# Outer-product recurrence and max-out layer on one core: another instruction order, two query steps in halves, one span turned by transfers

## The chip, the cores and the metric

The kernel runs on 1 core of one Trainium2 chip. The metric is the device time in microseconds (us) of one execution. The time of the kernel before is the median of three runs, 139.69 us (139.56 to 140.96).

## The reference

Two stages, one after the other. The first is a gated linear recurrence over 768 tokens for 4 batches, 8 heads and head size 48; the second is a max-out layer of 3072 tokens.

```python
f = 1.0 / (1.0 + np.exp(-f_logit))
for t in range(S):
    state = f[:, :, t, :, None] * state + np.einsum('bhd,bhe->bhde', k[:, :, t], v[:, :, t])
    y[:, :, t] = np.einsum('bhd,bhde->bhe', q[:, :, t], state)
x = y.transpose(0, 2, 1, 3).reshape(B * S, H * D)          # 3072 x 384
out = np.maximum(x @ w1, x @ w2) @ w_out                   # w1, w2 384 x 1024; w_out 1024 x 384
```

## The kernel before

The tokens are cut into 12 spans of 256 tokens: three windows of each of the four batches. Span s is window s // 4 of batch s % 4; a span is two chunks of 128 tokens, and each of the 128 partitions holds two neighbouring tokens ("parities"). Inputs of a span come as four loads of 384 KB (f, q, k, v) into 27 slots of SBUF. Spans 0 to 3 have no state at their start; later ones take the state of the span four before.

The max-out is rewritten: max(a, b) = b + relu(a - b). So the kernel forms wd = w1 - w2 once, and m2 = w2 @ w_out once; for each span it computes relu(x @ wd) @ w_out + x @ m2.

The whole program is one list of words, `ORDER`. A word is a step, its span or part, a letter for its engine where there is a choice (a ScalarE, v VectorE, p GpSimd, s SyncE) and after @ a PSUM bank or a slot. Each engine and each queue runs its own words strictly in the order in which they stand. Loads and stores all stand on SyncE's queue (SP). The words that matter here:

- Lf, Lk, Lq, Lv: the loads of a span. Wa0 to Wa3 (w1, 384 KB each), Wb0 to Wb2 (w2, 512 KB), Wo0 and Wo1 (w_out, 768 KB): the loads of the weights.
- E, F, G (ScalarE): gate, its logarithm, one factor. e: sum of a pair. C (TensorE): running sums. X and Z (ScalarE): the factors inv and dec. i, j: correction of the keys and the queries. K and Q: scaled keys (needs i and X) and queries (needs j and Z). V: values as bf16.
- t and u (TensorE): 16 transposes each, of the keys and of the queries; U: their copy out of PSUM (tile trs). A: scores of a half of the heads; m (VectorE): the masked scores. S and y: the outputs from the state and from within the span; z: a short read that keeps order. D, n, N: the state's update.
- Y: the outputs as bf16. For spans 6 to 10 (`TURNED`) Y goes to the tile xr, which has one buffer, and M turns it with a DMA transpose into xT. d: a quarter of x @ wd, 6 matmuls; r: relu; o: half of the output tokens, 11 matmuls over the rows of m2 and w_out; b: its copy out of PSUM; O: the store.
- wc, wt, wx: w2 as bf16, transposed, copied out. ws: a quarter of wd (needs a Wa and all three Wb). wo: a quarter of w_out as bf16. wm, wn: m2 and its copy. g: a memset of a state buffer.

Some rows of the profile have the line of a helper: L114 is the copy used by U, V, Y, b, wc, wx, wo and wn. Others: L247 step_i, L251 step_j, L258 step_K, L261 step_Q, L275 the transposes, L292 step_A, L299 step_m, L314 and L323 S and y, L387 step_D, L404 and L409 n and N, L427 step_M, L436 step_d, L461 step_o, L503 wm, L511 ws.

Of the kernel before, what the change touches and what calls it, by code (L numbers as in the profile page):

```python
# [12 lines left out]
BF16 = mybir.dt.bfloat16  # L13
# [7 lines left out]
Lf0s@16 g0v Lf1s@17 Lq0s@18 Lk0s@19 Lk1s@20 Lv0s@21 Lq1s@22 Wa2s E0 Wb1s F0 Lv1s@23 E1 e0v C0@0 F1  # L21
Wb2s j0v Z0 e1v X0 Q0v G0 C1@1 Wb0s i0v X1 u0@2 G1 g2v K0v Lf2s@24 i1p t0@2 U0.0v@2 U0.1a@3 Wa0s V0v
Z1 K1v D0@2 A0.1@0 Wa3s j1v A0.0@4 Q1v Wa1s m0.1v@0 u1@6 t1@6 Wo0s n0.0v U1.0a@6 U1.1a@7 Wo1s V1v
n0.1v D1@0 m0.0v@4 S0.0@2 A1.0@6 Lk2s@25 wc2a z0v@2 m1.0v@6 A1.1@4 S0.1 y0 Lq2s@26 wc0a ws2p n1.0v
n1.1v m1.1v@4 S1.0@6 Y0.0a@2 wt2@0 Lf3s@16 E2 g5p z1v@6 N1.1v S1.1 y1 N0.1p Lv2s@17 g3p ws0v wt0@1
Y1.1a@7 wx2a@0 Y0.1v@3 wc1p Lq3s@18 Y1.0v@6 d0.2@2 F2 g1p ws3v d0.0@4 Lk3s@19 wx0a@1 wt1@0 g4v e2v
d0.3@3 ws1v C2@1 r0.1a@2 d1.2@6 Lf4s@21 wo0v wx1v@0 wo1p d0.1@5 G2 d1.3@7 r0.0v@4 d1.0@2 Lv3s@20
wo2p wo3a d1.1@3 r1.1v@6 Z2 wm0@0 X2 g6v Lk4s@22 r1.0a@2 i2v wm1@1 K2v Lf5s@23 j2v wm2@2 Q2v Lq4s@24
E3 wn1v@1 t2@4 u2@4 F3 U2.0v@4 Lf6s@12 V2p wn2a@2 wn0v@0 o0.1@1 U2.1v@5 e3p A2.1@2 Lq5s@13 b0.1.0a@1
D2@4 A2.0@6 G3 n2.0v C3@0 j3v o1.1@1 Z3 n2.1v Lk5s@0 i3v X3 Q3v o1.0@0 m2.1v@2 E4 K3p F4 m2.0v@6  # L30
# [12 lines left out]
A7.0@0 b4.0.0v@2 A7.1@4 D7@6 N5.1p m7.0v@0 o5.0@3 Lq11s@19 K8p Lk11s@20 n7.0v O3.2s m7.1v@4 C9@2
N7.0p b5.0.0a@3 t8@0 Z9 u8@0 N6.1v S7.0@4 V8v X9 o5.1@3 U8.2v@0 V9a F11 n7.1v i9v D8@2 b5.1.0a@3
A8.1@0 z7v@4 N7.1p A8.0@6 n8.0v E10 m8.1v@0 d6.2@2 K9p d6.3@3 m8.0v@6 d6.0@0 r6.1a@2 N8.0p d6.1@1
Q9v S8.0@2 r6.0a@0 S7.1 y7 z8v@2 j11v t9@6 u9@6 e11v Y7.2a@4 S8.1 y8 U9.2v@6 C11@0 G11 M7s o6.1@1
F10 i11p Z11 Lk10s@23 X11 Q11p o6.0@4 Y8.2a@2 e10p A9.0@6 b6.0.0a@4 D9@0 M8s A9.1@2 K11p n9.0v
d7.1@5 m9.1v@2 C10@0 O5.2s d7.0@4 Z10 m9.0v@6 Lq10s@22 b6.1.0a@1 d7.3@3 Lv11s@12 G10 d7.2@2 O4.2s
r7.0a@4 N9.0v i10p Lv10s@24 d8.3@7 O6.2s X10 d8.1@5 r7.1a@2 K10v d8.2@6 d8.0@4 r8.1a@6 o7.1@1
r8.0a@4 j10v Q10p S9.0@2 t11@4 t10@6 z9v@2 u11@4 S9.1 y9 U11.0v@4 u10@6 U11.1v@5 o7.0@0 U10.2a@6  # L50
V11v V10v b7.1.0v@1 o8.1@4 Y9.2a@2 b7.0.0a@0 M9s D10@1 b8.1.0a@4 D11@0 O7.2s A11.0@2 A10.0@6 n11.0v
A11.1@4 m10.0v@6 o8.0@0 m11.1v@4 d9.0@6 N11.0v n10.0v d9.1@7 m11.0v@2 N10.0p d9.3@5 r9.0a@6 d9.2@4
b8.0.0v@0 O8.2s S10.0@0 r9.1a@4 S11.0@2 z10v@0 A10.1@6 z11v@2 S11.1 y11 m10.1v@6 S10.1 y10 Y11.0a@2
Y11.1a@3 o9.0@4 Y10.2a@0 M10s d11.2@5 b9.0.0v@4 d11.1@0 d11.3@1 o9.1@4 d10.1@3 b9.1.0v@4 r11.4a@5
# [6 lines left out]
M2_LAST = (0,)  # L61
TURNED = (6, 7, 8, 9, 10)


@with_exitstack
def kernel(
# [21 lines left out]
    DP = 64  # L88
# [174 lines left out]

    def step_V(s, e):
        copy(e, pad("vb", s)[:, :, :, 0:D], by_parity(loaded[s]["v"]))


    def transposes(s, x, b):
        src = pad("kpqp"[2 * x:2 * x + 2], s)
        for j in range(NP):  # L270
            for par in range(2):
                for h in range(2):
                    rows = slice(h * HC, (h + 1) * HC)
                    ps = banks16[:, b + h, :].rearrange("p (x j a t) -> p x j a t", x=2, j=NP, a=2)
                    nc.tensor.transpose(out=ps[:, x, j, par, :],  # L275
                                        in_=src[rows, par, 2 * j:2 * j + 2, :].rearrange("p r e -> p (r e)"),
                                        identity=ident[rows, rows])

    def step_U(s, part, e, b):
        t = tr[s] = buf("trs", s, 3, [C, 2, 2, NP, 2, HC], BF16)  # L280
        hs = slice(0, 2) if part == 2 else slice(part, part + 1)
        copy(e, t[:, hs].rearrange("p h x j a t -> p h (x j a t)"), banks16[:, b:b + hs.stop - hs.start, :])

    def step_A(s, jj, b):
        t = tr[s]
        for j in range(2 * jj, 2 * jj + 2):
            for par in range(2):
                for h in range(2):
                    for r in range(2):
                        rows = slice(r * DP, r * DP + D)  # L290
                        ps = banks[:, b + r, :].rearrange("p (j a t) -> p j a t", j=2, a=2)
                        nc.tensor.matmul(out=ps[h * HC:(h + 1) * HC, j % 2, par, :],  # L292
                                         lhsT=t[rows, h, 0, j, par, :],
                                         rhs=t[rows, h, 1, j].rearrange("p a t -> p (a t)"),
                                         start=True, stop=True, skip_group_check=True)
# [31 lines left out]
    def step_S(s, part, b):  # L327
        t = tr[s]
        if s in TURNED:
            ys[s] = b if part == 0 else ys[s]  # L330
            for j in range(NP):
                for r in range(2):
                    h = r if part else 1 - r
                    if has_state(s, h):
                        rows = slice(r * DP, r * DP + D)
                        add_turned(s, h, 2 * j + r, t[rows, h, 1, j].rearrange("p a t -> p (a t)"),
                                   heads_of(state_before(s, h))[rows, j, :], False)
            return
# [129 lines left out]
    def step_O(g, part):  # L468
# [3 lines left out]
        if g in TURNED:  # L472
            dst = out[row:row + W, :].rearrange("(h t a) m -> a t h m", h=2, a=2)
            for a in range(2):
                nc.sync.dma_start(out=dst[a], in_=obs[g][a * HC:(a + 1) * HC])
            return
        if g == n_s - 1 and part > 0:
            cols = slice((part - 1) * HD // 2, part * HD // 2)
            nc.sync.dma_start(out=dst[:, 1, cols], in_=obs[g][:, 1, cols])
            return  # L480
        pars = slice(0, 2) if part == 2 else slice(part, part + 1)
        nc.sync.dma_start(out=dst[:, pars, :], in_=obs[g][:, pars, :])
# [26 lines left out]
    def subtract(part, e):  # L509
# [15 lines left out]
        "t": lambda s, e, b: transposes(s, 0, b), "u": lambda s, e, b: transposes(s, 1, b),  # L525
        "U": lambda s, i, e, b: step_U(s, i, e, b),
# [3 lines left out]
        "Y": lambda s, i, e, b: step_Y(s, i, e, b), "g": lambda i, e, b: step_g(i, e), "M": lambda s, e, b: step_M(s, e),  # L530
        "D": lambda s, e, b: step_D(s, b),
# [3 lines left out]
        "O": lambda s, i, e, b: step_O(s, i),  # L535
# [4 lines left out]
    }  # L540
    for word in ORDER.split():
# [32 lines left out]
```

## Time and profile before

| | |
|---|---|
| median of three runs | 139.69 us |
| the profiled execution's own time | 141.23 us |
| its span | 139.5 us |
| TensorE busy | 119.1 us (85%) |
| VectorE busy | 101.7 us (73%) |
| ScalarE busy | 79.0 us (57%) |
| GpSimd busy | 45.3 us (32%) |
| read from HBM, written | 23.59 MB, 4.72 MB |
| granted TensorE clock | 1.0 throughout |

The span runs from the first to the last record of the profile; the execution's own time has 1.7 us more around it, and the profiled execution is 1.5 us above the median of the runs without a profile. TensorE's busy share counts overlapping matmuls as one stretch.

### The profile page before, as it was taken

The page shows a single profiled execution, that of the slowest core. Times are in us where ns is not written, and L with a number is a line of the kernel's source. Part 1 is how long each engine was busy: PE and PEld are TensorE (multiplying, and loading weights), DVE is VectorE, ACT ScalarE, POOL GpSimd, SP SyncE. Part 2 cuts the span into 40 slices and gives each one's busy share as a digit, 9 for nine tenths or more (in the row PEclk, how much of TensorE's full clock was granted, in tenths as well). Part 3 has the DMA queues.
Part 4 walks back from the last instruction along what each step waited for, and adds up shares of the span by engine and source line. Part 5 has one row for each costly group of instructions (what it writes and reads, how often), then busy time and mean ns, then how long its engine had stood idle before and what let it go on. Part 6 is the DMA issues. An engine that isn't in the chain of part 4 may idle for free. (4 is left out here: it accounts for less than half of the span.)

```text
span 139.5 us, 5551 instructions
## 1 busy us (share of the span) xinstructions
PE 119.1 (85%) x2455; PEld 89.5 (64%) x2455; DVE 101.7 (73%) x173; ACT 79.0 (57%) x120; POOL 45.3 (32%) x52
## 2 busy tenths in 40 slices
PE   0045489599999999999999699989999999999991
PEld 0024377586567687677787566776877668778671
DVE  5687798999889999989974989982642768312630
ACT  3784349665592996973983355693675814504301
POOL 5003007640538224482073096719635001000000
PEclk9999999999999999999999999999999999999999
DMA  4999999999999989999999999909899461422124
GB/s 109 271 261 296 348 332 349 369 267 251 269 265 257 271 222 273 239 248 250 247 297 222 224 274 163 288 30 96 121 260 313 130 140 34 118 56 61 57 62 164
DMA packets 59768, 29.65 MB, mean 213 GB/s; under 512 B 54368, under 2 KB 58592, under 8 KB 59744
## 3 DMA queue, kind: packets, MB, share of 16 engines
q1 hardware_dynamic: 59744, 29.30, 87.5%
q8 instruction: 19, 0.31, 1.0%
q14 instruction: 5, 0.04, 0.1%
HBM read 23.59 MB, written 4.72 MB: 203 GB/s over the span
## 5 line engine op out<-in xcount | busy, mean ns | idle before, releaser
L436 PE MATMUL banks<-xT,wd 128*128 128x256 bf16 x288 | 34.7, 273 | 2.3 <-DVE xT L114 2.0
L461 PE MATMUL banks<-wo,gT 128*128 128x384 bf16 (+1 forms) x200 | 35.3, 320 | 0.0
L436 PEld LDWEIGHTS <-wd 128*128 128x128 bf16 x288 | 27.2, 98 | 6.9 <-issue 2.3
L445 ACT ACTIVATE gT<-banks 128x1024 bf16<-128x1024 f32 (+1 forms) x20 | 19.5, 982 | 20.2 <-PE banks L436 15.7
L299 DVE TENSOR_TENSOR at_m<-banks,mask 128x1024 bf16<-128x1024 f32 x24 | 28.8, 1218 | 0.8 <-PE banks L292 0.5
L461 PEld LDWEIGHTS <-gT 128*128 128x128 bf16 x200 | 19.2, 98 | 11.8
L247 POOL TENSOR_TENSOR slots<-slots,one 128x384 f32<-128x384 f32 x8 | 8.5, 1058 | 28.1 <-DMA slots<-in_k_dram 18.3
L461 PE MATMUL banks<-m,xT 128*128 128x384 bf16 (+1 forms) x75 | 15.9, 320 | 0.0
L114 ACT COPY ob<-banks 128x384 f32<-128x384 f32 (+1 forms) x16 | 7.4, 460 | 11.9 <-PE banks L461 11.9
L114 DVE COPY trs<-banks 128x2048 bf16<-128x2048 bf16 (+1 forms) x12 | 11.9, 997 | 2.4 <-PE banks L275 2.3
L213 ACT ACTIVATE gate<-slots 128x768 f32<-128x768 f32 x12 | 10.1, 841 | 5.0 <-DMA slots<-in_f_logit_dram 5.0
L114 DVE COPY ob<-banks 128x384 f32<-128x384 f32 x9 | 5.0, 555 | 8.9 <-PE banks L461 8.9
L228 PE MATMUL banks<-e,u_inc 128*128 128x384 bf16 x12 | 4.2, 354 | 8.0 <-DVE e L224 8.0
L258 POOL TENSOR_TENSOR kp<-slots,inv 128x768 bf16<-128x768 f32 x5 | 9.6, 1913 | 3.0 <-DVE slots L247 2.9
L404 DVE TENSOR_TENSOR tmp_s<-banks,state 128x192 f32<-128x192 f32 x16 | 5.6, 352 | 6.7 <-ACT ob L114 3.9
L217 ACT ACTIVATE ell<-gate 128x768 f32<-128x768 f32 x12 | 10.1, 845 | 0.2
L292 PE MATMUL banks<-trs 48*64 48x128 bf16 x384 | 10.1, 234 | 0.0
L261 POOL TENSOR_TENSOR qp<-slots,dec 128x768 bf16<-128x768 f32 x4 | 7.3, 1817 | 8.3 <-PE banks L314 4.9
L251 DVE SCALAR_TENSOR_TENSOR slots<-gate,slots 128x384 f32<-128x384 f32 x12 | 6.6, 552 | 3.9 <-DMA slots<-in_q_dram 3.9
L114 ACT COPY trs<-banks 128x1024 bf16<-128x1024 bf16 (+1 forms) x4 | 4.8, 1227 | 7.0 <-PE banks L275 7.0
L292 PEld LDWEIGHTS <-trs 48*64 48x64 bf16 x384 | 7.5, 115 | 1.6 <-issue 1.1
L461 PEld LDWEIGHTS <-xT 128*128 128x128 bf16 x75 | 6.5, 97 | 3.2
(73 smaller groups left out, 186.3 us busy)
## 6 DMA issues: line engine op xcount, KB each, us to landing
slots<-in_f_logit_dram SPq DMA_DIRECT2D x12, 384.0 KB, 6.4
slots<-in_q_dram SPq DMA_DIRECT2D x12, 384.0 KB, 6.2
slots<-in_k_dram SPq DMA_DIRECT2D x12, 384.0 KB, 6.1
slots<-in_v_dram SPq DMA_DIRECT2D x12, 384.0 KB, 5.8
out_dram<-ob SPq DMA_DIRECT2D x6, 384.0 KB, 3.9
out_dram<-ob SPq DMA_DIRECT2D x11, 192.0 KB, 3.4
slots<-in_moe_w_dram SPq DMA_DIRECT2D x4, 384.0 KB, 8.7
slots<-in_moe_w_dram SPq DMA_DIRECT2D x3, 512.0 KB, 8.8
```

Source lines behind the costliest of these rows:

```text
L114: (nc.scalar.copy if e == "a" else engines[e].tensor_copy)(out, in_)
L213: nc.scalar.activation(flat(gate[s]), flat(loaded[s]["f"]), AF.Exp, bias=0.0, scale=-1.0)
L217: nc.scalar.activation(flat(ell[s]), flat(gate[s]), AF.Ln, bias=1.0, scale=1.0)
L247: engines[e].tensor_mul(even, even, one[s])
L251: engines[e].scalar_tensor_tensor(out=even, in0=gate[s][:, :, 1, :], scalar=1.0, in1=even, op0=ALU.add, op1=ALU.mult)
L258: engines[e].tensor_mul(pad("kp", s)[:, :, :, 0:D], by_parity(loaded[s]["k"]), both(inv[s]))
L261: engines[e].tensor_mul(pad("qp", s)[:, :, :, 0:D], by_parity(loaded[s]["q"]), both(dec[s][:, 0:HD].rearrange("p (h d) -> p h d", h=H)))
L292: nc.tensor.matmul(out=ps[h * HC:(h + 1) * HC, j % 2, par, :], lhsT=t[rows, h, 0, j, par, :], rhs=t[rows, h, 1, j].rearrange("p a t -> p ( ...
L299: nc.vector.tensor_mul(at[s][:, jj].rearrange("p r j a t -> p (r j) (a t)"), banks[:, b:b + 2, :].rearrange("p r (j x) -> p (r j) x", j=2) ...
L436: nc.tensor.matmul(out=ps[:, f], lhsT=wd[:, kt, ff * C:(ff + 1) * C], rhs=xT[g][:, kt], start=(kt == 0), stop=(kt == KT - 1))
L445: nc.scalar.activation(dst, src, AF.Relu)
L461: nc.tensor.matmul(out=ps, lhsT=lhs, rhs=rhs, start=(i == 0), stop=(i == len(terms) - 1))
```

## The change

`ORDER` is written anew, and some words are new.

- Spans 0 and 1: step Q on all eight heads becomes two steps q of four heads each (q0.0, q0.1, q1.0, q1.1), the transposes u become uq (8 each), and the copy U has the parts 3 (all keys), 4 and 5 (the queries of half the heads).
- Span 11: t11, u11 and both U11 are gone. Mk11 and Mq11 turn its scaled keys and queries with a DMA transpose each (128 x 1024, bf16) from SP's queue straight into trs; `key_t` and `query_t` hand the turned pieces to A and S.
- A step on GpSimd of the kinds in `SHARED` waits for the last such step of VectorE that stands ahead of it in the list.
- The stores O7, O8, O9 and the last piece of O11 are issued by ScalarE.
- Everything has a new place, and many steps another engine. Word for word, GpSimd loses four e, three i, two K, three Q and three V, and takes one K, two Q, two V, one q, five N (against three), a ws, and more g.

```diff
+SHARED = ("e", "i", "j", "K", "Q", "q", "V", "N", "ws", "wc", "wo")
 TURNED = (6, 7, 8, 9, 10)
+BY_DMA = (11,)
...
+    def step_q(s, jj, e):
+        hs = slice(4 * jj, 4 * jj + 4)
+        sums = dec[s][:, 0:HD].rearrange("p (h d) -> p h d", h=H)[:, hs]
+        engines[e].tensor_mul(pad("qp", s)[:, :, hs, 0:D], by_parity(loaded[s]["q"])[:, :, hs],
+                              sums.unsqueeze(1).to_broadcast([C, 2, 4, D]))
...
+        if part > 2:
+            x, js = (0, slice(0, NP)) if part == 3 else (1, slice(2 * part - 8, 2 * part - 6))
+            src = banks16[:, b:b + 2, :].rearrange("p h (x j y) -> p h x j y", x=2, j=NP)
+            copy(e, t[:, :, x, js].rearrange("p h j a t -> p h (j a t)"),
+                 src[:, :, x, js].rearrange("p h j y -> p h (j y)"))
+            return
...
+    def step_turn(s, x, e):
+        t = tr[s] = buf("trs", s, 3, [C, 2, 2, NP, 2, HC], BF16)
+        src = pad("kpqp"[2 * x:2 * x + 2], s).rearrange("p two h e -> p (two h e)")
+        engines[e].dma_start(out=whole(t)[:, x], in_=src, transpose=True)
...
+    def key_t(s, rows, h, j, par):
+        if s in BY_DMA:
+            return whole(tr[s])[rows, 0, NP * par + j, h * HC:(h + 1) * HC]
+        return tr[s][rows, h, 0, j, par, :]
...
-                nc.sync.dma_start(out=dst[a], in_=obs[g][a * HC:(a + 1) * HC])
+                engines[e].dma_start(out=dst[a], in_=obs[g][a * HC:(a + 1) * HC])
...
+        if key in SHARED and e in ("v", "p"):
+            ins = nc.cur_bb.bb.instructions[-1]
+            if e == "v":
+                ahead = ins.name
+            elif ahead:
+                tc.add_manual_dep(ins, ahead, mybir.DependencyInfo(mybir.DependencyClass.Sync,
+                                                                   mybir.DependencyReason.DATA),
+                                  reason="as listed")
```

The parts of the two lists that the prediction speaks of, taken apart by engine:

```
SP before:  f0 f1 q0 k0 k1 v0 q1 Wa2 Wb1 v1 Wb2 Wb0 f2 Wa0 Wa3 Wa1 Wo0 Wo1 k2 q2 f3 v2 ...
SP after:   f0 f1 k0 Wb2 q0 q1 v0 f2 Wb0 Wb1 k1 Wa1 Wa0 v1 Wa3 Wa2 Wo1 f3 Wo0 q2 k2 v2 ...
            ... M6 v10 k11 v11 v9 M7 q10 M8 Mq11 O4 Mk11 O6 M9 O5 M10 O10 O11.0 O11.1
PE before:  C0 C1 u0 t0 D0 A0 A0 u1 t1 D1 S0.0 A1 A1 S0.1 y0 S1.0 wt2 S1.1 y1 wt0 d0.2 d0.0
            wt1 d0.3 C2 d1.2 d0.1 d1.3 d1.0 d1.1 wm0 wm1 wm2 t2 u2 ...
PE after:   C0 t0 wt2 C1 uq0.0 uq0.1 A0 A0 uq1.1 uq1.0 D0 S0.0 S0.1 y0 wt0 t1 wt1 C2 A1.1 d0.0
            d0.1 A1.0 D1 d0.3 S1.0 S1.1 y1 d0.2 d1.3 d1.1 d1.2 d1.0 C3 wm2 wm1 wm0 u2 t2 ...
            ... y7 S8.1 y8 o6.0 C10 o6.1 C11 d7 D9 A9 A9 o7.0 d8 S9.0 u10 t10 S9.1 y9 o7.1
            A10.1 D11 A11.1 A10.0 D10 o8.0 d9 ...
DVE after:  ... m0.1 q1.1 m0.0 n0.0 z0 n0.1 K1 U1.4 ws1 e2 ws0 Y0.0 wx1 m1.1 m1.0 n1.0 n1.1 z1
            wo2 Y1.0 e3 wo0 r0.1 j2 Q2 i2 K2 U2.1 ...
ACT after:  ... U0.5 U0.4 Z1 X1 E2 U1.5 F2 Y0.1 wc1 U1.3 wx0 r0.0 Z2 G2 X2 Y1.1 E3 F3 wo1 ...
            ... X10 Z10 Y8 Z11 b6.1 X11 r7.1 ...
POOL after: g5 g2 g0 q1.0 g6 g4 wc0 i1 N0.1 V1 ws3 ws2 wo3 Q3 ... i11 K11 Q10 N9.0 N11.0
```

More of the change, by code (lines that the diff above doesn't have):

```diff
@@ L26 @@
[L26 to L30, printed above, removed]
@@ L43 @@
[L43 to L48, printed above, removed]
@@ L49 @@
[L49 to L54, printed above, removed]
@@ new lines @@
+i11p S7.1 y7 S8.1 y8 U9.2a@6 N7.1v e10v o6.0@4 Y7.2v@2 e11v M7s i10v C10@5 o6.1@2 V10v X10 Lq10s@24
+j11v Z10 K10v C11@3 b6.0.0v@4 V9v Y8.2a@0 d7.3@7 d7.2@6 Z11 M8s b6.1.0a@2 Q11v d7.0@0 X11 r7.1a@6
+d7.1@1 K11p Mq11s D9@2 r7.0a@0 A9.1@4 A9.0@6 o7.0@3 O4.2s j10v Mk11s m9.1v@4 Q10p d8.3@1 O6.2s
+m9.0v@6 d8.2@0 d8.0@4 n9.0v r8.1a@0 N9.0p d8.1@5 S9.0@0 r8.0a@4 u10@6 t10@6 z9v@0 V11v S9.1 y9
+U10.2a@6 o7.1@2 Y9.2v@0 M9s b7.0.0a@3 A10.1@0 b7.1.0v@2 D11@3 A11.1@4 O5.2s A10.0@6 n11.0v O7.2a
+D10@2 m10.1v@0 N11.0p o8.0@3 m11.1v@4 d9.2@0 n10.0v m10.0v@6 d9.1@5 d9.3@1 d9.0@4 r9.1v@0 o8.1@2
@@ L466, in step_b, with step_O @@
         copy(e, obs[g][:, par, cols], banks[:, b, cols])
-    def step_O(g, part):
+    def step_O(g, part, e):
         w, b = divmod(g, B)
@@ L525 @@
         "t": lambda s, e, b: transposes(s, 0, b), "u": lambda s, e, b: transposes(s, 1, b),
+        "uq": lambda s, i, e, b: transposes(s, 1, b, range(2 * i, 2 * i + 2)),
+        "q": lambda s, i, e, b: step_q(s, i, e),
         "U": lambda s, i, e, b: step_U(s, i, e, b),
@@ L540 @@
     }
+    ahead = None
     for word in ORDER.split():
```

94 lines of the change are left out of this document (59 added, 35 removed).

## The prediction

> **What bounds the kernel now.** I read the page first, then the busy time of four stretches of the span, then the timeline of the first 37 us.
>
> ```profile
> span 139.5 us, 5551 instructions
> PE 119.1 (85%) x2455; PEld 89.5 (64%) x2455; DVE 101.7 (73%) x173; ACT 79.0 (57%) x120; POOL 45.3 (32%) x52
> ```
>
> ```profile
> 0.00:27.00 27.00, 12.12 (x349) 10.47 (x350) 21.61 (x51) 16.23 (x22) 7.77 (x18) 1.00 1.07 289
> 27.00:36.50 9.50, 9.50 (x109) 7.16 (x108) 9.08 (x15) 5.78 (x9) 2.12 (x3) 1.00 1.08 271
> 36.50:136.60 100.10, 97.47 (x2000) 71.85 (x1998) 70.98 (x109) 56.64 (x90) 35.36 (x32) 1.00 0.83 189
> 136.60:139.50 2.90, 0.00 (x0) 0.00 (x0) 0.00 (x0) 0.31 (x1) 0.00 (x0) 1.00 0.36 129
> ```
>
> The columns are stretch, length, then busy time of PE, PEld, DVE, ACT, POOL, the granted clock, the DMA share and GB/s. TensorE is idle for 14.9 of the first 27 us, then works without a gap until 36.5 and loses only 2.6 us in the 100 us after that. The last 2.9 us are one copy and the last store. In the first 27 us the transfers are never idle (share 1.07). So the time is: when TensorE gets going, plus its own work, plus small gaps, plus the tail. An edit counts if it lets TensorE do more before about 30 us, takes work off TensorE later, or opens or closes gaps. TensorE enters its unbroken stretch so:
>
> ```profile
> 25.83 1.47 PE L436 MATMUL banks<-xT,wd 128*128 128x256 bf16 x12 [1.64 <-DVE xT L114]
> ...
> 28.51 3.43 PE L436 MATMUL banks<-xT,wd 128*128 128x256 bf16 x30
> 31.78 4.06 PE L503 MATMUL banks<-wo,slots 128*128 128x384 bf16 x24
> ```
>
> The thirty matmuls at 28.51 are d1.2, d0.1, d1.3, d1.0 and d1.1, 0.114 us each; the last row is the product m2. If d0.1 (0.69 us) had been done ahead, as in the new order, span 1's d steps would have begun at 29.2. That is the mark which the new order has to meet.
>
> **The start, step by step.** When loads land is read from the steps that waited for them:
>
> ```profile
> 7.46 0.56 DVE L251 SCALAR_TENSOR_TENSOR slots<-gate,slots 128x384 f32<-128x384 f32 x1 [0.70 <-DMA slots<-in_q_dram]
> 10.60 1.15 POOL L247 TENSOR_TENSOR slots<-slots,one 128x384 f32<-128x384 f32 x1 [8.06 <-DMA slots<-in_k_dram]
> 21.48 1.04 ACT L114 CAST slots<-slots 128x1024 bf16<-128x1024 f32 x1 [0.28 <-DMA slots<-in_moe_w_dram]
> 24.18 1.03 DVE L511 TENSOR_TENSOR wd<-slots 128x768 bf16<-128x768 f32 x1 [0.47 <-DMA slots<-in_moe_w_dram]
> 28.39 0.84 POOL L114 CAST wo<-slots 128x768 bf16<-128x768 f32 x1 [1.84 <-DMA slots<-in_moe_w_out_dram]
> 30.49 0.83 ACT L114 CAST wo<-slots 128x768 bf16<-128x768 f32 x1 [0.61 <-DMA slots<-in_moe_w_out_dram]
> ```
>
> From q0 (7.46) to k1 (10.60) two loads of 384 KB landed, 1.57 us each; from Wo0 (28.39) to Wo1 (30.49) one of 768 KB, 2.1 us. The new order keeps the volume and changes who comes first. k1 was fifth and lands eleventh: through k1 the queue now holds what the old one held through Wb0 (21.48), with f2 in place of v1 and without Wa2, so it lands one load earlier, about 20.2. By adding single loads from the start it would be 19.2. Wo0 now lands last, after f3: one load after 30.49, about 32.0.
>
> What follows k1 is a chain on three engines: i1 on GpSimd (1.15, in the row of 10.60), K1 on VectorE, then VectorE's words in their order. GpSimd has wc0 ahead of i1, and that waits for Wb0, so i1 ends no earlier than about 20.9; with k1 at 20.2 it is 21.4. I take K1's start at 21.2. VectorE's durations:
>
> ```profile
> L258 DVE TENSOR_TENSOR kp<-slots,inv 128x768 bf16<-128x768 f32 x7 | 6.6, 945 | 1.1 <-POOL slots L247 1.0
> L224 DVE TENSOR_TENSOR e<-ell 128x384 bf16<-128x384 f32 x6 | 3.2, 541 | 0.8 <-ACT ell L217 0.8
> L114 DVE COPY slots<-banks 128x1024 bf16<-128x1024 bf16 x1 | 0.7, 678 | 0.0
> L299 DVE TENSOR_TENSOR at_m<-banks,mask 128x1024 bf16<-128x1024 f32 x24 | 28.8, 1218 | 0.8 <-PE banks L292 0.5
> L404 DVE TENSOR_TENSOR tmp_s<-banks,state 128x192 f32<-128x192 f32 x16 | 5.6, 352 | 6.7 <-ACT ob L114 3.9
> L114 DVE CAST wo<-slots 128x768 bf16<-128x768 f32 x1 | 1.2, 1175 | 0.0
> L114 DVE CAST m<-banks 128x384 bf16<-128x384 f32 x2 | 1.1, 550 | 0.0
> ```
>
> ```profile
> 41.31 2.35 DVE L299 TENSOR_TENSOR at_m<-banks,mask 128x1024 bf16<-128x1024 f32 x2
> ```
>
> K1 0.95; U1.4, half of a copy of 1024, 0.4 (between 0.34 and 0.68 by the copy row); ws1 and ws0 1.03 each; e2 0.54; Y0.0 0.55 (the copy of 384 values from PSUM); wx1 0.68; m1.1 and m1.0 1.22 each; n1.0 and n1.1 0.35 each; wo2 1.18; Y1.0 0.55: together 10.1. Two m back to back take 2.35 and not 2.44, so each step but the last saves 0.09, about 1.1 over thirteen. Y1.0 ends at 21.2 + 9.0 = 30.2, and d1 starts there against the mark of 29.2: **1.0 us lost**. With K1 at 20.9 it is 0.7; if a weight load holds up ws1 or ws0 it is 2. Nothing else TensorE has in its order covers it: d0.0, d0.1, A1, D1, y1 and d0.2 are done by then, and m2 stands behind d1.
>
> The halved queries do work: the first half of span 0 is turned before the second is scaled, so span 0's outputs come earlier. But d0 stands on TensorE behind t1 and A1.1, which hang on k1, so that lead goes into waiting, and I cost it at nothing; at best it makes up the 1.0.
>
> d1 is done at 30.2 + 24 x 0.114 = 32.9, and C3 stands between it and m2 (moved from behind m2, so not added). wo0 needs Wo0 at 32.0 plus its cast of 1.18: 33.2. So m2 starts with no or little wait, 0.1; if f3 costs more than one load, a wait of up to 1 us.
>
> **Later parts.** Taking t11 and u11 off TensorE is read from the chain that ended last, and so is the price of a DMA transpose:
>
> ```profile
> 93.56 3.95 DMA xT<-xr
> ...
> 98.43 3.77 DMA xT<-xr
> ...
> 102.25 2.79 PE banks L436 x24
> 105.04 1.79 PE banks L461 x11
> ...
> 107.03 0.70 PE banks L275 x48
> ```
>
> Forty-eight transposes took 0.70, so thirty-two give back **0.5 us**. The U11 copies leave VectorE, which is not the bound there. Against it stand two more transfers on SP, 1024 columns where M7 and M8 had 768, so by 4/3 of 3.8 about 5 us from issue to landing. They must land before A11.1. Counted from M7's landing: TensorE has d7 and d8 (2.8 each), o7.0 and o7.1 (1.8 each) and about 2.6 us of D9, A9, S9, u10, t10, y9, A10.1 and D11 ahead of A11.1, 11.8 us. Mk11 waits for Y8, Z11, b6.1 and X11 on ScalarE, then K11 on GpSimd:
>
> ```profile
> L114 ACT CAST xr<-banks 128x768 bf16<-128x768 f32 x4 | 3.2, 803 | 2.1 <-DMA xT<-xr 2.1
> L243 ACT ACTIVATE dec<-banks 128x392 f32<-128x392 f32 x12 | 5.9, 494 | 2.5 <-PE banks L231 2.5
> L258 POOL TENSOR_TENSOR kp<-slots,inv 128x768 bf16<-128x768 f32 x5 | 9.6, 1913 | 3.0 <-DVE slots L247 2.9
> ```
>
> 0.8 + 3 x 0.5 + 1.9 = 4.2, and 5 to land: 9.2, with 2.6 to spare. I cost the transfers at nothing; SP carries M8, Mq11 and O4 ahead of Mk11, and that is the slow rival. d7 itself waits for M7: o6.0 and o6.1 (3.6) with S8, y8 and two C, about 5, stand against Y7 (0.95, as K of the same size) and 3.9 of transfer; I add 0.3, between 0 and 1.
>
> **The waits of GpSimd** have a reason in the trace:
>
> ```profile
> 51.46 1.03 POOL L247 TENSOR_TENSOR slots<-slots,one 128x384 f32<-128x384 f32 x1 [4.18 <-DMA slots<-in_k_dram]
> 51.54 1.16 DVE L409 TENSOR_TENSOR state<-tmp_s,dec 128x192 bf16<-128x192 f32 x1
> ```
>
> ```profile
> L409 DVE TENSOR_TENSOR state<-tmp_s,dec 128x192 bf16<-128x192 f32 x9 | 5.1, 568 | 0.0
> ```
>
> That N, a small product, took 1.16 us and ended just after GpSimd's step; undisturbed it is near the 0.35 of n. Over nine N that is 2.0 us of VectorE. The Trainium skill (GPSIMD Engine Reference, section Key points) says that GpSimd shares its SBUF interfaces with VectorE and contends with VectorE instructions that have two SBUF inputs; this row agrees. By it alone the waits would give VectorE up to those 2.0 us. Since TensorE is busy 97.5 of 100.1 us beside it, I take none of it, and bound the gain by the 2.6 us of gaps, the loss by as much again: a GpSimd step now queued behind a late VectorE step delays its followers (K after i, then t).
>
> The stores moved to ScalarE: it was busy 57%, and the last store still begins after the last copy. I cost them at nothing. The Trainium skill (Trainium Kernel Development and Optimization, section Key Constraints) has it that issuing from several engines only saves the sequencer's issue time; no run here shows that yet.
>
> **The sum** against the profiled span: 139.5 + 1.0 + 0.1 - 0.5 + 0.3 = 140.4. The profiled execution's own time is 141.23, 1.5 above the median of the runs without a profile; I put the difference, +0.9, on the median 139.69: **140.6 us**.
>
> **The rivals.**
> - *Faster, 137.4.* The d1 mark is met (k1 earlier, or wc0 quicker: the 1.0 and 0.1 are gone), the transposes give 0.5, and the 2.0 us of contention on VectorE closes most of the 2.6 us of gaps, 1.8. 139.69 - 2.3 = 137.4. For it: VectorE is busy 9.1 of 9.5 us where TensorE starts. Against: in the 100 us after, only 71 of 100.
> - *Slower, 142.7, span 11's transfers.* If a transpose holds SP's transfers for its whole time to landing, M8 lands 4.7 after M7, Mq11 9.7, O4 10.9, Mk11 16, and A11.1, with o8 and d9 behind it in TensorE's order, waits 4.2 us. Half of that, for transfers that overlap in part, gives 140.6 + 2.1 = 142.7. It decides from the point where Mk11 lands later than 11.8 us after M7.
> - *No change, 139.7.* The waits bind nowhere since GpSimd is behind anyway, the new order only trades gaps, and start and transposes cancel.
>
> **How the numbers follow.** Forecast 0.43 (own range 139.5 to 142.0), faster 0.22, span 11 late 0.20, no change 0.15. A measurement of this kernel tells about 1% from no change: below 138.3 and above 141.1. Faster: 0.20 of the second, 0.02 each of forecast and no change, 0.24. Slower: all of span 11 late, 0.14 of the forecast (its upper part, a weight load that holds up ws), 0.02 of no change, 0.36. The rest, 0.40, is within 1%. The range reaches to the faster case and past the slow one, 137.4 to 143.5.
>
> **What would show it.** Right: d1 and m2 start 1 us later than now, GpSimd's step_i at about 20 us waits for k1's load, no gap ahead of A11.1, TensorE's gaps after 37 us again near 2.6 us. Wrong: d1 at 29 or earlier; VectorE's state products at 0.35 us and gaps well under 2 us; or a gap of over 1 us that ends with trs from a DMA.

## The result and the profile after

The changed kernel is a little slower: 141.90 us median of 15 runs (140.66 to 143.25) against 140.52 us (139.11 to 141.96, 15 runs) of the kernel before on the same chip. The ratio is **1.0107 [1.0078, 1.0136]**. The forecast was 140.6 us, a loss of 0.9 us on the 139.69 us it started from; the ratio makes it 1.5. The ratios here and below leave out executions that are more than 1.5% above the fastest of the same kernel.

The page of the kernel after, its span and engines, and the busy time of the four stretches that were shown of before (same columns):

```profile
span 139.4 us, 5485 instructions
PE 119.8 (86%) x2423; PEld 89.0 (64%) x2423; DVE 100.8 (72%) x174; ACT 85.3 (61%) x126; POOL 36.5 (26%) x47
```

```profile
0.00:27.00 27.00, 13.23 (x303) 10.56 (x304) 20.91 (x51) 14.41 (x22) 10.30 (x23) 1.00 1.06 286
27.00:36.50 9.50, 8.37 (x116) 6.16 (x116) 6.05 (x12) 6.35 (x12) 2.32 (x2) 1.00 1.11 277
36.50:136.60 100.10, 98.21 (x2006) 72.30 (x2004) 73.79 (x113) 64.54 (x95) 23.93 (x23) 1.00 0.84 195
136.60:139.50 2.90, 0.00 (x0) 0.00 (x0) 0.00 (x0) 0.03 (x1) 0.00 (x0) 0.99 0.29 100
```

The first thing to see is that the spans hide the loss: 139.4 after, 139.5 before. The profile of before that the prediction was built on came from an execution 1.5 us above its median, with gaps at 78 and 93 us of 0.71 and 0.52 that a second profile of the same kernel does not have. That second one has a span of 137.9, a second one of after again 139.4, and their difference, 1.5, is near that of the medians, 1.4. So before and after are compared from here on by the second profiles, *before again* and *after again*.

The loss lies ahead of 36.5 us: by 27.0 TensorE has passed 303 matmuls instead of 349, and in the second stretch, where it had 9.50 us of work in 9.50, it now has 8.37. The timeline of TensorE in *before again*, where it enters the product m2 and where it ends:

```profile
28.26 3.44 PE L436 MATMUL banks<-xT,wd 128*128 128x256 bf16 x30
31.53 4.06 PE L503 MATMUL banks<-wo,slots 128*128 128x384 bf16 x24
...
134.17 0.82 PE L461 MATMUL banks<-wo,gT 128*128 128x192 bf16 x8
```

The same in *after again*:

```profile
30.07 0.52 PE L344 MATMUL banks<-at_m,vb 64*64 64x128 bf16 x18 [0.73 <-issue]
34.14 4.06 PE L541 MATMUL banks<-wo,slots 128*128 128x384 bf16 x24
...
135.44 0.82 PE L499 MATMUL banks<-wo,gT 128*128 128x192 bf16 x8
```

m2 starts at 34.14 instead of 31.53, **2.6 us later**; 0.3 of that is C3, which now stands ahead of it. From m2 to the end of the last matmul it is 102.1 us instead of 103.5 (135.44 + 0.82 - 34.14 against 134.17 + 0.82 - 31.53), so **1.3 come back**. The tail is 3.1 instead of 2.9. The sum is 2.6 - 1.3 + 0.2 = 1.5.

The first row of after again is what no part of the prediction had: in the middle of y1, between two matmuls of the same step, TensorE stood for 0.73 us, and the profile names no releaser ("issue"). The experiments ask where the 2.6 us come from, whether the waits of GpSimd and span 11's transfers cost or give anything, and what that stop is.

### The profile page after: what moved, and what is told of

It is laid out like the page before. It is cut to its first block, busy times and chain, and to the rows that moved or that the text cites. A ratio compares the mean times of both kernels' runs of the same rounds, so it can differ in the third digit from the quotient of the medians.

```text
span 139.4 us, 5485 instructions
## 1 busy us (share of the span) xinstructions
PE 119.8 (86%) x2423; PEld 89.0 (64%) x2423; DVE 100.8 (72%) x174; ACT 85.3 (61%) x126; POOL 36.5 (26%) x47
## 4 chain that ended last, share of the span: by engine, by line
PE 72%; DVE 9%; DMA 6%; ACT 6%; issue 3%; POOL 1%; DVEq 0%; POOLq 0%
PE banks L499 25%; PE banks L474 23%; PE banks L344 6%; PE banks L283 4%; PE banks L323 4%; DMA xT<-xr 3%; PE banks L352 3%; DMA slots<-in_f_logit_dram 3%; PE banks L425 2%; PE banks L541 2%; DVE trs L116 2%; PE banks L529 1%; DVE kp L260 1%; POOL qp L263 1%; ACT ell L219 1%
## 5 line engine op out<-in xcount | busy, mean ns | idle before, releaser
L499 PEld LDWEIGHTS <-gT 128*128 128x128 bf16 x200 | 19.2, 98 | 11.8
L116 ACT COPY trs<-banks 128x2048 bf16<-128x2048 bf16 (+2 forms) x10 | 13.0, 1314 | 5.8 <-PE banks L283 5.8
L485 DVE TENSOR_SCALAR gT<-banks 128x1024 bf16<-128x1024 f32 x5 | 6.1, 1219 | 6.1 <-PE banks L474 6.0
L263 POOL TENSOR_TENSOR qp<-slots,dec 128x768 bf16<-128x768 f32 x3 | 5.4, 1816 | 17.6 <-DVE slots L253 12.5
L116 DVE COPY ob<-banks 128x384 f32<-128x384 f32 (+1 forms) x10 | 5.3, 534 | 6.1 <-PE banks L499 6.1
L260 POOL TENSOR_TENSOR kp<-slots,inv 128x768 bf16<-128x768 f32 x4 | 7.3, 1815 | 9.5 <-DVE qp L263 7.0
L260 DVE TENSOR_TENSOR kp<-slots,inv 128x768 bf16<-128x768 f32 x8 | 7.9, 991 | 1.0 <-POOL slots L249 0.4
L344 PE MATMUL banks<-at_m,vb 64*64 64x128 bf16 x336 | 7.8, 231 | 0.7 <-issue 0.7
L447 POOL TENSOR_TENSOR state<-tmp_s,dec 128x192 bf16<-128x192 f32 x9 | 4.8, 536 | 13.6 <-DVE tmp_s L442 5.8
L253 DVE SCALAR_TENSOR_TENSOR slots<-gate,slots 128x384 f32<-128x384 f32 x12 | 7.6, 636 | 0.9 <-DMA slots<-in_q_dram 0.9
L249 POOL TENSOR_TENSOR slots<-slots,one 128x384 f32<-128x384 f32 x5 | 5.0, 999 | 11.9 <-DVE e L226 5.3
```

Of the source, the lines that this page charges most:

```text
L116: (nc.scalar.copy if e == "a" else engines[e].tensor_copy)(out, in_)
L253: engines[e].scalar_tensor_tensor(out=even, in0=gate[s][:, :, 1, :], scalar=1.0, in1=even, op0=ALU.add, op1=ALU.mult)
L260: engines[e].tensor_mul(pad("kp", s)[:, :, :, 0:D], by_parity(loaded[s]["k"]), both(inv[s]))
L263: engines[e].tensor_mul(pad("qp", s)[:, :, :, 0:D], by_parity(loaded[s]["q"]), both(dec[s][:, 0:HD].rearrange("p (h d) -> p h d", h=H)))
L344: nc.tensor.matmul(out=to if len(rhs.shape) == 2 else to.rearrange("p (a t) -> p a t", a=2), lhsT=lhs[:, at_col + off:at_col + off + DP], ...
L499: nc.tensor.matmul(out=ps, lhsT=lhs, rhs=rhs, start=(i == 0), stop=(i == len(terms) - 1))
```

## The experiments

### The two kernels again, and the waits of GpSimd

*Both kernels again*, unchanged, for a second profile:

> The kernel before, unchanged: a second profile, since its first profiled execution (141.23 us) was slower than its median (140.52). Expected: m2 starts at 31.8 us again; what differs from the first profile lies after it, in gaps of TensorE that one execution has and the other has not.

> The changed kernel, unchanged: a second profile, since its first profiled execution (141.25 us) was faster than its median (141.9). Theory A (the start) expects m2 at 34.2 us again and a span of 139.4 to 140.4; if the loss lies in the rest, a gap appears there that the first profile did not have.

Measured: before 0.9997 [0.9964, 1.0031], after 1.0095 [1.0060, 1.0131]. The profiles are the ones read above: the start of after is no accident of one execution (m2 at 34.20 and 34.14), the gaps at 78 and 93 us in the first profile of before were one.

*The new order without the waits:*

```diff
-SHARED = ("e", "i", "j", "K", "Q", "q", "V", "N", "ws", "wc", "wo")
+SHARED = ()
```

> The changed kernel without the added waits of GpSimd on VectorE. Theory A (the loss arises at the start, where m2 begins 2.1 us later than before when C3 is set aside): the waits cost nothing, so the ratio to the kernel before stays near 1.010, within 0.3 us of the changed kernel. Theory B (the waits hold GpSimd's steps back, and K and t behind them): the ratio falls to 1.000 to 1.003.

Measured: **1.0317 [1.0254, 1.0379]**. Without the waits the new order is another 2.1%, 2.9 us, slower, so both theories missed: they had the waits at nothing or as a cost, and here they are a gain. *The old order with them* (before's list, after's code and `SHARED`):

> The old order with the new rule alone: every GpSimd step of the shared kinds waits for the VectorE step ahead of it in the list. Theory W (a GpSimd step that starts early holds VectorE up until it ends, which cost 2.9 us in the changed kernel without the waits): the mean of VectorE's state products falls from 0.57 to near 0.4 us and the ratio is 0.990 to 0.998. Rival (the rule only helps an order that was laid out for it): 1.000 to 1.010, since steps i and K on GpSimd start later.

Measured: 1.0011 [0.9982, 1.0041]; there they change nothing, as the rival had it. One place in the timelines of VectorE and GpSimd shows what the waits prevent. First no_waits, with the row of TensorE that follows from it:

```profile
48.71 2.98 DVE L447 TENSOR_TENSOR state<-tmp_s,dec 128x192 bf16<-128x192 f32 x2
48.58 1.00 POOL L249 TENSOR_TENSOR slots<-slots,one 128x384 f32<-128x384 f32 x1 [3.95 <-DMA slots<-in_k_dram]
49.66 1.81 POOL L260 TENSOR_TENSOR kp<-slots,inv 128x768 bf16<-128x768 f32 x1
52.21 0.34 PE L230 MATMUL banks<-e,u_inc 128*128 128x384 bf16 x1 [1.57 <-DVE e L226]
```

Then the kernel after:

```profile
48.69 0.62 DVE L447 TENSOR_TENSOR state<-tmp_s,dec 128x192 bf16<-128x192 f32 x2
49.90 0.99 POOL L249 TENSOR_TENSOR slots<-slots,one 128x384 f32<-128x384 f32 x1 [5.29 <-DVE e L226]
50.98 1.81 POOL L260 TENSOR_TENSOR kp<-slots,inv 128x768 bf16<-128x768 f32 x1
```

The same two state products of span 2 and 3 take 0.62 us when GpSimd waits (its releaser is VectorE's e), and 2.98 when i4 and K4 run beside them: they end at 51.69, just after K4 (51.47). e5 comes behind them on VectorE, and TensorE waits 1.57 us for it with its running sums. m2 starts at the same 34.2 us in both kernels; from there to the last matmul TensorE's gaps are 5.1 us in no_waits and 1.6 in after, and this wait is the largest of them. Over the whole span the groups of N say the same (before again, after, no_waits, old order with waits):

```profile
L409 DVE TENSOR_TENSOR state<-tmp_s,dec 128x192 bf16<-128x192 f32 x9 | 3.8, 422 | 0.0
L447 DVE TENSOR_TENSOR state<-tmp_s,dec 128x192 bf16<-128x192 f32 x7 | 3.1, 458 | 0.0
```

```profile
L447 DVE TENSOR_TENSOR state<-tmp_s,dec 128x192 bf16<-128x192 f32 x7 | 5.6, 809 | 0.0
```

```profile
L447 DVE TENSOR_TENSOR state<-tmp_s,dec 128x192 bf16<-128x192 f32 x9 | 4.0, 444 | 0.0
```

In the old order the mean is 0.57 and 0.42 us in the two profiles without the waits and 0.44 with them. So against the old order the waits are not a gain: they repair a cost that the new order has without them.

### Span 11 turned by transfers, and the stores

*The new order with t11, u11 and the U11 back on TensorE and VectorE:*

```diff
-BY_DMA = (11,)        # and Mq11, Mk11 out of the list
+BY_DMA = ()           # t11@4 u11@4 behind t10, U11.2v@4 behind U10.2
```

> The changed kernel with span 11's keys and queries turned by TensorE again (t11, u11 and one U11 copy, no transfers). Theory A: TensorE gets its 0.5 us of transposes back, the ratio to the kernel before rises from 1.010 to about 1.014. Theory C (the two transfers, or what stands behind them on the queue, cost the time): the ratio falls to 1.005 or less, and the 0.5 us gap ahead of the last d steps closes.

Measured: 1.0155 [1.0047, 1.0262]. That holds both 1.0107 and half a per cent more, so it does not decide. *The old order with span 11 by transfers* (t11, u11, U11.0 and U11.1 out, Mq11 and Mk11 behind the load of v10, no waits):

> The old order with span 11's keys and queries turned by two transfers behind the last load of v, and t11, u11 and both U11 copies gone; nothing else. Expected by the step of the prediction: 0.5 us of TensorE saved, the transfers hidden, ratio 0.994 to 0.999. Rival (the transfers delay the stores and M9 behind them on the queue): 1.003 or more, with a gap of TensorE ahead of A11 or of d9.

Measured: 1.0008 [0.9973, 1.0043]. The 0.5 us of the prediction is not seen in the time, and is not excluded: the interval is that wide. TensorE's work shows it. From the start of m2 to the last matmul, before again and before_11dma, then after again and eleven_pe (columns as above):

```profile
31.53:134.99 103.46, 101.93 (x2058) 74.69 (x2055) 74.85 (x116) 59.81 (x94) 35.73 (x32) 1.00 0.81 195
31.57:134.74 103.17, 101.53 (x2026) 74.24 (x2023) 73.13 (x114) 59.77 (x94) 35.87 (x32) 1.00 0.84 200
```

```profile
34.14:136.27 102.13, 100.37 (x2024) 73.62 (x2021) 75.11 (x116) 66.79 (x97) 24.19 (x23) 1.00 0.84 195
35.76:140.20 104.44, 101.08 (x2056) 74.06 (x2053) 76.56 (x116) 66.55 (x97) 23.91 (x23) 1.00 0.78 183
```

Without the 32 transposes TensorE has 0.4 us less to do in the old order and 0.7 in the new one. The transfers hold nothing up. In the kernel after, SP's own queue and the first scores of span 11 on TensorE:

```profile
100.12 1.23 SPq L304 DMA_TRANSPOSE trs<-qp  x1
102.07 1.45 SPq L304 DMA_TRANSPOSE trs<-kp  x1
...
109.96 0.63 PE L323 MATMUL banks<-trs 48*64 48x128 bf16 x30
```

Mk11 is issued at 102.07 and lands 5.0 us later by the table of transfers; A11.1 starts at about 110 with no wait named.

*The four stores back on SP's queue:*

```diff
-O7.2a ... O8.2a ... O9.2a ... O11.2a
+O7.2s ... O8.2s ... O9.2s ... O11.2s
```

> The changed kernel with O7, O8, O9 and the last piece of O11 issued by SP again, at the same places of the list. By the prediction these moves cost nothing: ratio 1.008 to 1.013. Rival (ScalarE's copies wait behind its own stores, 2.4 us in the profile after, and the tail is 0.2 us longer): 1.005 or less.

Measured: 1.0128 [1.0087, 1.0169], beside 1.0107 of after: no difference is seen between the two engines that issue them.

### The start alone

Two kernels were to part the start from the rest: before's list up to m2 and after's from there, and the other way round.

> The old order up to the product m2, then the changed kernel's order for all the rest, with its waits and its transfers for span 11. Theory A: the 2 us lost at the start come back and the rest of the new order is as good or better, so the ratio to the kernel before is 0.990 to 1.000 (139.1 to 140.5 us). Theories B and C (the loss lies in the rest): 1.008 or more.

> The mirror image: the changed kernel's order up to m2, then the old order for all the rest, without waits and without transfers for span 11. Theory A: the start loses its 2 us and nothing gives any of it back, ratio 1.012 to 1.018. Theories B and C: 1.000 to 1.003.

Measured: 1.0181 [1.0124, 1.0238] and 1.0479 [1.0396, 1.0562]. In the first X2 reads a PSUM bank that m2 has already been written to, in the second r1.1 does. So both compute something else than the layer, each of these steps waits for m2, and their times hold stops of their own (in the first, TensorE waits 1.21 us for e3 and 1.02 at 47.98). Both are inconclusive: their times can't be put down to the halves.

*y1 brought forward*, by taking what stood ahead of it on TensorE and VectorE out of the way:

```diff
-... A1.1 d0.0 d0.1 A1.0 D1 d0.3 S1.0 S1.1 y1 d0.2 ...      (VectorE: n1.0 n1.1 z1)
+... A1.1 A1.0 d0.0 d0.1 D1 S1.0 S1.1 y1 d0.3 d0.2 ...      (VectorE: n1.0 z1 n1.1)
```

> The changed kernel with three words moved: A1.0 ahead of d0.0, n1.1 behind z1, d0.3 behind y1. Theory A: y1 and so d1 and m2 come about 0.5 us earlier (m2 at 33.7), ratio 1.004 to 1.008. Rival: the stop of 0.7 us in the middle of y1 moves along and m2 stays at 34.2, ratio 1.010.

Measured: 1.0216 [1.0148, 1.0284]. Three of the six executions took 141.8 to 142.0 us; in the other three, 143.7 to 144.0, the granted clock fell (last section), so this ratio can't be set beside the 1.0107 of after, and the starts of m2 are compared instead: 34.63 us here, 34.20 in after. The timeline of TensorE in y1_early:

```profile
28.04 0.24 PE L344 MATMUL banks<-trs,state 48*64 48x128 bf16 x2 [0.25 <-DVE look L395]
30.07 0.42 PE L344 MATMUL banks<-at_m,vb 64*64 64x128 bf16 x12 [1.15 <-issue]
34.63 4.06 PE L541 MATMUL banks<-wo,slots 128*128 128x384 bf16 x24
```

y1 began half a microsecond earlier, the stop in it grew from 0.73 to 1.15, and it went on at the same 30.07. d0.3, now behind y1, then came on top. That is the rival's account, with m2 0.4 us later still. So the waits for A1.0, z1 and r0.0 ahead of y1, which looked like the cause, are not what sets its end.

*Span 1 served first:* its k and v loaded ahead of f2 and two of w2's rows, i1 right behind q1.0 on GpSimd and K1 behind m0.0 on VectorE, and d's quarters taken in the order in which wd's come.

```diff
-Lq0 Lq1 Lv0 Lf2 Wb0 Wb1 Lk1 Wa1 Wa0 Lv1 ...    g6p ... i1p ... S0.1 y0 N0.1p ... K1v ... t1
+Lq0 Lq1 Lv0 Lk1 Lv1 Lf2 Wb0 Wb1 Wa1 Wa0 ...    i1p ... g6p ... K1v ... V1p ... D0 ... S0.0 t1 ... S0.1 y0
-d0.0 d0.1 ... d0.3 ... y1 d0.2 d1.3 d1.1 d1.2 d1.0
+y1 d0.1 d1.1 d0.0 d1.0 d0.3 d1.3 d0.2 d1.2
```

> The changed kernel with span 1 served earlier at the start: k1 and v1 load ahead of f2 and the rows of w2, and i1, K1, t1, A1, D1 and y1 stand earlier on their engines; all from r0.1 on is as in the changed kernel. Theory A (the loss is span 1's late outputs, which hold d1 and m2): m2 starts at 32.5 to 33 us in place of 34.2 and the ratio falls from 1.0107 to 0.997 to 1.003. Rival D (what is won at the start is eaten again by the steps behind m2, which wait for loads): m2 is earlier, but the ratio stays at 1.007 or more.

Measured: 1.0437 [1.0388, 1.0485]. Theory A missed, and rival D has the ratio but not the path, since m2 is later and not earlier. Its timeline, TensorE's and a GpSimd row:

```profile
29.99 3.51 PE L474 MATMUL banks<-xT,wd 128*128 128x256 bf16 x24 [0.65 <-issue]
33.97 2.78 PE L474 MATMUL banks<-xT,wd 128*128 128x256 bf16 x24 [0.46 <-ACT gT L483]
28.93 3.89 POOL L549 TENSOR_TENSOR wd<-slots 128x768 bf16<-128x768 f32 x2 [7.16 <-DVE wd L549]
```

y1 is over before 29.4 here, and still the next matmul does not come before 29.99. Behind it a new chain opens: w2's rows land later, so two quarters of wd on GpSimd wait 7.16 us for VectorE's and end at 32.8, r0.0 and the gates E3 and F3 come late behind d0.0, and m2 starts at 37.4. In this profile the granted clock is 0.50 from 28.1 to 31.5 us, which alone stretches the end of y1 and the first d; executions at a clock of 1.0 took 144.9 and 146.4 us, so the loss stays without it.

### What the stop is

The count of matmuls up to a stop, in the column behind PE, is the same in every kernel that has it. Stretches from 0 to just before TensorE goes on: after, y1_early, span1_early, then after and no_waits later in the span:

```profile
0.00:30.10 30.10, 15.23 (x351) 11.90 (x351) 22.79 (x55) 15.60 (x24) 12.62 (x24) 1.00 1.07 291
```

```profile
0.00:30.05 30.05, 15.11 (x351) 11.60 (x351) 23.05 (x55) 15.61 (x24) 12.60 (x24) 1.00 1.07 292
```

```profile
0.00:29.98 29.98, 13.64 (x351) 11.12 (x351) 21.96 (x55) 15.27 (x24) 9.84 (x22) 0.97 1.08 291
```

```profile
0.00:93.50 93.50, 77.51 (x1759) 57.84 (x1759) 77.35 (x140) 67.94 (x102) 31.92 (x43) 1.00 1.09 269
```

```profile
0.00:75.50 75.50, 58.13 (x1247) 42.26 (x1247) 62.42 (x113) 51.69 (x78) 23.24 (x35) 1.00 1.04 262
```

351, 1247 and 1759 are each 95 and a multiple of 128, and so is 223, behind which after again stopped 0.52 us at 23.88. The 352nd matmul is in y1 in after, six later in y1 in y1_early (d0.3's six were moved behind it), and the first of a d in span1_early. In all eight profiles with the new start and without extra matmuls, the 352nd begins between 29.99 and 30.36 us. The table of DMA queues has two of kind "instruction"; one of them, q8, has 19 packets of 16 KB, and behind the first 95 of the 2423 matmuls there are 19 blocks of up to 128. In the trace of after the packets of q8 around the start are at 21.38 to 22.62 and 27.54 to 28.72; TensorE went on behind matmul 223 at 23.93 and behind 351 at 30.13, 1.3 and 1.4 us after a packet had landed. In y1_early the second landed at 28.64 and TensorE went on at 30.07, in span1_early at 28.65 and 29.99, in no_waits (behind 1247) at 74.13 and 75.57. In before again the packets landed at 18.43 and 25.03, and TensorE passed 223 and 351 at 20.15 and 26.90, after they were due: no stop there. Later in the span the first profile of before has one too, 0.52 us behind 1759.

So TensorE's instructions come in blocks of 128 matmuls with their weight loads, by transfers that share the DMA engines with the loads, and around the start a new block is fetched some 4 us after the one before is begun: from passing 95 to the packet that lets 224 go it is 4.2 us in after (21.38 - 17.19), from 223 to the next 3.6 (27.54 - 23.93), and with the packet's 1.2 and the 1.4 behind it 6.2 to 6.7 in all. The old order passes 95 at 13.75 and 351 at 26.90, 13.2 us for two blocks. The new order passes 95 at 17.19, 3.4 later, and has work ready for 351 at 29.19, 12.0 later; the supply took 12.9.

*The test* moves the edges of the blocks by 80 extra transposes at the very start, of a constant into a bank that nothing reads:

```diff
+    for _ in range(80):
+        nc.tensor.transpose(out=banks16[:, 7, 0:HC], in_=ident[0:HC, :], identity=ident[0:HC, 0:HC])
     ahead = None
     for word in ORDER.split():
```

> The kernel after with 80 extra transposes of 64 rows at the very start of TensorE's order, of a constant into bank 7, which nothing reads; by the rows of t0 (16 in 0.61 us) they take about 3 us and lie in the idle time before the first running sums at 6.8 us. No other word moves.
>
> What the traces so far show: in every kernel the stops named issue come after exactly 223, 351, 1247 or 1759 matmuls, that is 95 and a multiple of 128, whatever the 352nd matmul is (in y1, six later in y1 when d0.3 was moved behind it, or the first of a d).
>
> Theory, instructions come in blocks of 128 matmuls, and a block can run no earlier than about 6.3 us after the block before it was begun, while the loads run: the 80 move the edges of the blocks to what were the 143rd and the 271st matmul, which TensorE passed at about 19.2 and 26.0 us, 6.8 apart, with the edge before them at 10.7. So the stop of 0.73 us in y1 and the one of 0.2 to 0.5 in C2 at 23.9 go, y1 ends at about 29.9, d1 starts at 30.5, m2 at 33.4 instead of 34.1, and the time is about 0.7 us below the kernel after: 1.005 of before (1.002 to 1.008), with 80 instructions more. A stop that is left stands again behind 95 and a multiple of 128 matmuls by the new count.
>
> Rival, the stop belongs to the time (what the transfers do at 30 us) or to y1: it stays in y1, ends again at 30.0 to 30.4 us, and the ratio is that of the kernel after, 1.010, or a little more for the extra instructions.

Measured: 1.0145 [1.0021, 1.0269], six executions from 140.86 to 144.20 us, median 143.35 against 140.38 of before: it is not told apart from 1.0107, and it is no faster. The trace tells more. TensorE's timeline in after_80more (y1's first and last rows, what follows, and three stops later), and the count up to the first and the last of these:

```profile
30.08 0.24 PE L344 MATMUL banks<-trs,state 48*64 48x128 bf16 x2 [0.25 <-DVE look L395]
...
30.23 0.87 PE L344 MATMUL banks<-at_m,vb 64*64 64x128 bf16 x44
31.04 3.51 PE L474 MATMUL banks<-xT,wd 128*128 128x256 bf16 x30
...
69.58 0.38 PE L283 MATMUL banks<-ident,qp 64*128 64x64 bf16 x14 [0.62 <-issue]
75.22 0.32 PE L344 MATMUL banks<-at_m,vb 64*64 64x128 bf16 x9 [0.61 <-issue]
97.47 0.48 PE L499 MATMUL banks<-m,xT 128*128 128x384 bf16 x2 [1.53 <-issue]
```

```profile
0.00:69.50 69.50, 57.61 (x1247) 43.64 (x1248) 56.44 (x108) 47.53 (x74) 20.13 (x31) 1.00 1.10 274
```

```profile
0.00:97.30 97.30, 83.37 (x1887) 63.40 (x1888) 79.02 (x143) 69.29 (x102) 31.90 (x43) 1.00 1.04 259
```

The stops in C2 and in y1 are gone, and y1 runs through in 1.0 us. But y1 begins only at 30.08 here, when the stop in after was nearly over, so y1 by itself does not rule out a stop that belongs to the time. The new stops do: they stand behind 1247, 1375 and 1887 matmuls of the new count, other work than before at the same multiples, and TensorE goes on 1.5 to 1.7 us after a packet of q8 has landed at each. That is what the theory of blocks says and the rival does not. The time that the expectation hung on it did not come: in the profiled execution k1 landed 1.4 us later (i1, the row below, starts at 20.29; in after at 18.91), which moved y1 by about as much (30.08 for 28.57), and the three new stops, 2.8 us, took the place of one of 0.5 at 93.5. So the cause of the stop is shown; that removing it would give 0.7 us is not.

```profile
20.29 1.00 POOL L249 TENSOR_TENSOR slots<-slots,one 128x384 f32<-128x384 f32 x1 [1.71 <-DMA slots<-in_k_dram]
```

No version beat the kernel before: the nearest, the old order with span 11 by transfers and the old order with the waits, equal it.

## Why the prediction was right, and where it was not

**The sum.** Its level is near for reasons that in part cancel. It has the start at a loss of 1.1 us (1.0 and 0.1) and the rest at a gain of 0.2 (0.5 less 0.3). Measured, with C3 set aside on both sides, the start lost 2.3 and the rest gave back 0.8 (1.3 less C3's 0.3, less 0.2 of tail). The two are off by 1.2 and by 0.6 in opposite directions; that the sum is only 0.6 from the measured 1.5 is to that extent luck.

**The bound and the mark.** Right: the time is set by when TensorE enters its unbroken stretch. The mark, d1 at 29.2, and the sign of the miss were right; before again, which begins m2 0.25 us earlier, has it at 28.95.

**The chain to Y1.0.** This term was mis-sized, 2.1 us instead of 1.0: d1 starts at about 31.3. k1 landed at about 18.9, nearer to the 19.2 that the prediction set aside than to the 20.2 that it took; VectorE's own rows in after, K1 and m1.0 at its two ends, then z1 and Y1.0:

```profile
19.94 1.25 DVE L260 TENSOR_TENSOR kp<-slots,inv 128x768 bf16<-128x768 f32 x1 [0.44 <-POOL slots L249]
26.42 1.22 DVE L328 TENSOR_TENSOR at_m<-banks,mask 128x1024 bf16<-128x1024 f32 x1 [0.50 <-PE banks L323]
28.36 0.16 DVE L395 COPY look<-banks 128x1 f32<-128x1 f32 x1
30.69 0.56 DVE L116 CAST xT<-banks 128x384 bf16<-128x384 f32 x1 [1.70 <-PE banks L344]
```

K1 began at 19.94 and not at 21.2, but took 1.25 and not 0.95, and m1.0 waited 0.50 for A1.0; it was done at 27.64, by the sum's own terms 28.1. The step that failed is the one that took Y1.0 as the next word of VectorE's list: it waits for y1, 1.70 us, and y1 is TensorE's. y1 began at 28.57 behind z1, and its instructions were not there until 30.13. Without that stop (0.94 us from 29.19 to 30.13) d1 would have begun near 30.4, by this estimate near the 30.2 of the prediction, and that too by two errors against each other: K1 too late, the wait for y1 left out. "Nothing else TensorE has in its order covers it" was true, but the sum asked only what TensorE has to do, not when its instructions come.

**m2 behind d1.** Right: m2 follows C3 without a wait, wo is there. Where d1 is late, m2 is as late.

**Transposes and U11 off the engines, 0.5.** Right as work of TensorE, 0.4 and 0.7 us in the two pairs of profiles above; in the time it is not separated, since 0.5 us is as wide as the interval of before_11dma. From m2 on TensorE has 1.6 us less work than before (100.37 for 101.93) and 0.2 more gaps, which gives the 1.3 that come back; 0.3 of it is C3's place, 0.4 to 0.7 the transposes, and the rest is not attributed. Waiting for a turned Y was put at 0.3, at d7 for M7; in after it is 0.47, and at d10:

```profile
123.70 5.40 PE L474 MATMUL banks<-xT,wd 128*128 128x256 bf16 x48 [0.47 <-DMA xT<-xr]
```

**The waits of GpSimd at nothing.** Right as a comparison of the two kernels, since TensorE's gaps did not shrink: from m2 to the last matmul they are 1.8 us in after and 1.5 in before by the second profiles (102.13 less 100.37, 103.46 less 101.93). The prediction's sign for this, gaps again near 2.6 us, did not come, because the 2.6 were those of one execution of before.

It was wrong as a price: in the new order the waits are worth 2.9 us. The prediction bounded a gain by the gaps that the old order has, and an order with more such collisions has more to lose. The Trainium skill (GPSIMD Engine Reference, section Key points) says that GpSimd contends with VectorE instructions that have two inputs in SBUF; N is one, and its rows of 0.62 and 2.98 us agree.

**The stores at nothing.** Right, by sync_stores. The Trainium skill (Trainium Kernel Development and Optimization, section Key Constraints) has it that issuing from several engines only saves the sequencer's time; 1.0128 [1.0087, 1.0169] beside 1.0107 agrees.

**The rivals.** Span 11's transfers were on time. The faster case needed the d1 mark, which was missed. "No change" missed by the start.

**The base.** The sum was made against an execution 1.5 us above its median and moved to the median of three runs by one difference. Of the 1.3 us between the forecast of 140.6 and 141.90, 0.8 is the base itself, which 15 executions put at 140.52. And the first profile's gaps of 2.6 us, on which the faster rival rests, were 1.5 in the second.

## What to carry to other kernels

Follow the chain of a late step through the engine that feeds it as well, and where a stop in the middle of one engine's work is named "issue", count its instructions up to the stop before looking for a cause in the data: if the counts agree between kernels, it is the supply of instructions. Two steps on GpSimd and VectorE that are free to meet can each be cheap and cost microseconds together; whether an ordering wait is worth something depends on the list it is put in, so it is tried in the list that will run. Take a second profile of the base before attributing a difference of one per cent.

## What the runs showed of the hardware that was not expected

- TensorE's instructions come in blocks of 128 matmuls with their weight loads (stops behind 223, 351, 1247, 1375, 1759 and 1887), 16 KB each, over the DMA engines. In the loaded start of this kernel a block could run 6.2 to 6.7 us after the one before was begun (at the later stops 3.0 to 5.9), so many small matmuls in a row (351 of them in the first 30 us) can outrun it; the d steps, 0.114 us a matmul and so 14.6 a block, do not.
- What GpSimd costs VectorE is a wait and not a share. In no_waits the two N of the rows above end at 49.80 and 51.69 us, each 0.22 us after a GpSimd step (i4 at 49.58, K4 at 51.47), and the one in the prediction's row ends 0.21 after; alone an N takes 0.35. In before an N that began in the same moment as i (101.35) took 0.35, and the GpSimd step 1.21 instead of 1.03. The product n, which reads PSUM, takes 0.35 us beside GpSimd as well as alone.
- The page gives the granted clock as 1.0 from the first record, but TensorE is slower near the start: in after the sixteen transposes of the keys take 0.61 us at 21.99 (span 1) and 0.40 at 38.44 (span 2). A rate of TensorE that is read later in the span is too fast for the start.
- In some executions the granted clock fell to 0.50 for 3.4 us, which neither profile of before shows while TensorE has work. Stretches of span1_early and of eleven_pe (PEclk is the third from the end):

```profile
30.00:33.00 3.00, 3.00 (x21) 2.42 (x22) 1.16 (x2) 0.11 (x1) 3.00 (x3) 0.75 1.21 263
```

```profile
30.00:33.00 3.00, 2.64 (x27) 1.96 (x28) 0.56 (x1) 1.69 (x3) 0.10 (x1) 0.50 1.15 255
```

One such fall costs half of 3.4 us and makes the mean clock of an execution of 140 us 0.988. That mean stands beside 4 of the 23 executions of after (142.6 to 143.7 us, the others 140.7 to 142.2), 3 of 6 of y1_early and 2 of 6 of the old start with the new rest; in the 68 executions of before that were run beside the experiments it is never under 0.997. So this is a cost of some new orders that the prediction had no term for. Why the clock falls is open: in the 3.4 us ahead of the fall in eleven_pe TensorE was busy for 2.0 us, and in after, which kept its clock, for 2.0 in the same place.
